# A spectral layer and a token/channel mixer: 940 more columns by seven block products, their groups narrowed earlier and partly on GpSimd

## The chip, the core and the metric

The kernel runs on one core of a Trainium2 chip. The core has a matrix engine (TensorE, in the profile PE for matmuls and PEld for weight loads), VectorE (DVE), ScalarE (ACT), GpSimd (POOL) and a queue processor, SyncE (SP), that here only issues DMAs. SBUF is on-chip memory with 128 partitions, PSUM holds matmul results. The metric is the device time of one execution in microseconds; the kernel before takes 2310.04 us, the median of three runs (2308.27 to 2310.43).

## What is computed

Two parts follow each other, on x of shape (8 batches, 3008 positions, 256 channels):

```python
X = np.fft.rfft(x, axis=1)
Yr = Xr @ w_r - Xi @ w_i + b_r
Yi = Xr @ w_i + Xi @ w_r + b_i
Y = soft_threshold(Yr, 0.01) + 1j * soft_threshold(Yi, 0.01)
y = np.fft.irfft(Y, n=3008, axis=1)            # a
h = np.maximum(y.T @ w_tok1, 0) @ w_tok2       # over positions, 3008 -> 256 -> 3008
u = y + h.T
out = u + np.maximum(u @ w_ch1, 0) @ w_ch2     # over channels, 256 -> 1536 -> 256
```

The weights of the second part arrive as float64. They are read as pairs of 32-bit words and narrowed on the chip to float32 (`narrow`): two ScalarE operations and six that were all on VectorE.

## The kernel before

A position n is written by two indices, of 47 and of 64, and the Fourier transform is done as two short transforms by matmul (`stage1`, `forward`, `inverse`). Where full float32 precision is wanted, an operand is split into a high part in float32r and the remainder, and a product is three matmuls (`mm3`); the split is a copy (mostly ScalarE) and a subtraction (VectorE or GpSimd).

The batches are worked in five units: batch 0 alone, batch 1 alone, then three pairs (`UNITS`, line 24). The *spectral work* of a unit gives blocks b_d in DRAM and a matrix g (the relu of the token product, as gh and gl). From these, a *group* of up to 470 positions of u is made by `half_u`, once for each half of the 256 channels: six matmuls with the group's piece of w_tok2 (tile wt2: high and low parts of two halves, 470 or 376 columns) and one product with a block of b_d (tile b2) for each slot of 94 positions. Unit 0 has seven groups of 470, 376, 376, 376, 470, 470 and 470 columns. For unit 0 the piece of w_tok2 is loaded as float64 (`load_wt2`), narrowed (`narrow_wt2`), split (`split_wt2`), used, and kept in DRAM (`keep_wt2`, tensor wt2_d); the later units load it from there.

The *channel mixing* takes u in chunks of columns. A chunk up to 512 columns wide is done by `channel`: 12 blocks f of the 1536 hidden values, each with a first product (6 matmuls, PSUM tile ph), a relu on ScalarE (hh) and its remainder on VectorE (hlo), and two steps later a second product (6 matmuls, accumulated in PSUM tile po): 144 matmuls. A wider chunk is done in the tail by `channel7`: its columns and the hidden blocks are cut into halves, and a 2 x 2 block product is made with seven products instead of eight in each layer. A step is one of 6 pairs of hidden blocks: seven products of three matmuls for the first layer and seven for the second, 42 matmuls over half the chunk's columns. The sums of columns (tiles t and ub) are made by `first_u`, `rest_u` or `sums_u`, the sums of weights (ws, ws2) by `weigh` and `weigh2` during the last narrow chunk, and `replace` puts sums in place of a quarter of the weights.

Before the change unit 0 has seven narrow chunks, one for each group; unit 1 has wide chunks of 960, 1024 and 1024 columns, each pair 896 and five of 1024.

The order of the work is this:

- `begin` (line 774): the spectral work of batch 0 in plain float32, the narrowing of w_tok1, w_ch1 and of the first pieces of w_ch2, group 0, and the first steps of unit 1's spectral work (each `extra(1)`).
- The loop at line 1445 goes through the narrow chunks. After each step f of `channel` it takes as many steps of the spectral work as a pace asks: the unit-1 work left over the channel work left, from the first chunk to the one ahead of the last narrow one. Unit 1's steps also carry the first transform of unit 2 (`jobs`).
- Ahead of the last narrow chunk ("end") the rest of the spectral work, units 2 to 4, runs by itself, with `wc["pure"]` set; in it `mix` takes its PSUM from the pool ps1 under the tag po.
- Then comes the last narrow chunk, with the sums of weights, and the tail.

In a narrow chunk n the group of the next chunk is prepared at fixed steps: loads at f = 1 and 3, narrowing at 3 and 5, splits at 4 and 6, `make_u` at 9. In the last narrow chunk the three groups of the first wide chunk are made at f = 4, 7 and 10. Outside the tail the framework orders the instructions on each engine by their dependencies and its own estimates when the program is built; in the tail PE keeps the order that is written (ORDER and TURN in `channel7`: O for products of the second layer of the step before, N for the first layer of the new step). Group halves stand between the tail's steps, at places listed in `when`; the tiles wt2 and b2 have one buffer each. Loads run on SP's queue, most stores on ScalarE's (PUT).

## Time and profile before

| what | us |
| --- | --- |
| median of three runs | 2310.04 |
| profiled execution | 2313.43 |
| its span in the trace | 2311.2 |
| PE busy (matmul) | 2273.5 (98%) |
| DVE busy | 1718.8 (74%) |
| ACT busy | 1476.2 (64%) |
| POOL busy | 1389.7 (60%) |

Busy time is from the page of the profiled execution. Matmuls overlap and their ends are modelled, so a busy PE is not PE at its peak; the price of a matmul is better read from the distance between the starts of two. In time the stages lie as follows, by the last relu of the first layer and the last addition of each chunk: `begin` up to 155 us, the first six narrow chunks with unit 1's spectral work to about 446, the spectral work alone to about 858, the last narrow chunk to 906, the tail to the end. Rows of the order of time give start, length, engine, line, operation, output and inputs, shapes, and in brackets the idle time ahead with what ended it; rows of waits give total, times and the longest; rows of groups give count, busy time, mean nanoseconds, idle time.

### The profile page before, as it was taken

To read this page: it belongs to the slowest core of one execution; us is meant where nothing else is said; L and a number is where in the kernel's file an instruction comes from. 1 tells how busy PE (TensorE), PEld (TensorE's weight loads), DVE (VectorE), ACT (ScalarE), POOL (GpSimd) and SP (SyncE) were. 2 spreads that over 40 slices of the span, in tenths; PEclk is the share of its full clock that TensorE was granted. 3 is DMA by queue.
4 is the path that set the end of the run, shared out by engine and by line. 5 is a ranking of instruction groups with operands and counts; after the bars stand their busy time and mean duration, and the time that the engine had idled before them with its cause. 6 is when DMAs were issued, how large, how long until landed. Compare 5 with 4: busy or idle time off the path is not lost.

```text
span 2311.2 us, 34802 instructions
## 1 busy us (share of the span) xinstructions
PE 2273.5 (98%) x12092; PEld 1976.0 (85%) x12092; DVE 1718.8 (74%) x2806; ACT 1476.2 (64%) x2700; POOL 1389.7 (60%) x1119
## 2 busy tenths in 40 slices
PE   8999999999999999999999999999999999999998
PEld 7879999989989988888988888898888889888876
DVE  7967776577887667777777777777777777777877
ACT  6755554455655445776676777667777766767776
POOL 0000223344553333887787888778788877878885
PEclk9999999999999999999999999999999999999999
DMA  8876576787876542122222212222221122222201
GB/s 209 262 241 182 144 215 186 236 260 251 263 241 217 178 153 85 42 81 69 85 62 69 64 37 67 70 85 62 69 65 42 61 69 85 62 69 64 59 1 37
DMA packets 150958, 277.22 MB, mean 120 GB/s; under 512 B 11078, under 2 KB 95390, under 8 KB 150782
## 3 DMA queue, kind: packets, MB, share of 16 engines
q1 hardware_dynamic: 115241, 208.40, 30.2%
q10 hardware_dynamic: 35540, 66.60, 8.5%
q8 instruction: 96, 1.57, 0.3%
q14 instruction: 81, 0.66, 0.1%
HBM read 177.57 MB, written 97.39 MB: 119 GB/s over the span
## 4 chain that ended last, share of the span: by engine, by line
PE 82%; DVE 9%; DMA 3%; issue 2%; ACT 1%; POOL 1%; SPq 1%; ACTq 0%; DVEq 0%; POOLq 0%
PE l L134 15%; PE sx L134 14%; PE sz L134 11%; PE sy L134 10%; PE sw L134 7%; PE px L497 3%; PE pm L208 2%; PE pm L210 2%; PE pm L209 2%; PE gp L210 1%; PE gp L208 1%; PE gp L209 1%; DMA raw<-in_wt 1%; DVE ts L1216 1%; PE gp L578 1%
## 5 line engine op out<-in xcount | busy, mean ns | idle before, releaser
L1213 POOL TENSOR_TENSOR op<-ts,op 128x512 fp32r<-128x512 f32 (+2 forms) x503 | 638.0, 1290 | 245.0 <-ACT op L1246 241.4
L1246 ACT ACTIVATE op<-ts 128x512 fp32r<-128x512 f32 (+2 forms) x504 | 311.2, 619 | 63.5 <-DVE ts L1216 48.2
L1213 DVE TENSOR_TENSOR uf<-sy,uf 128x512 f32<-128x512 f32 (+2 forms) x232 | 156.3, 674 | 223.6 <-PE sy L134 223.2
L134 PE MATMUL l<-op,ws 128*128 128x512 f32 (+2 forms) x1134 | 314.3, 385 | 0.0
L134 PEld LDWEIGHTS l<-op,ws 128*128 128x128 f32 x1134 | 212.9, 188 | 40.1
L1242 ACT ACTIVATE x<-sx 128x512 f32<-128x512 f32 (+2 forms) x252 | 148.5, 589 | 139.2 <-PE sx L134 138.7
L134 PE MATMUL sx<-ub,w 128*128 128x512 f32 (+2 forms) x756 | 211.7, 388 | 1.9 <-DVE ts L1216 1.0
L134 PE MATMUL sx<-ub,ws 128*128 128x512 f32 (+2 forms) x756 | 209.8, 386 | 0.5 <-ACT x L1242 0.5
L161 POOL TENSOR_TENSOR yl<-z,yh 128x512 fp32r<-128x512 f32 x72 | 96.3, 1337 | 126.0 <-ACT yh L158 118.2
L134 PEld LDWEIGHTS sx<-ub,w 128*128 128x128 f32 x756 | 141.7, 188 | 31.5 <-DVE ts L1216 3.2
L134 PEld LDWEIGHTS sx<-ub,ws 128*128 128x128 f32 x756 | 141.8, 188 | 27.8 <-ACT x L1242 0.9
L1213 POOL TENSOR_TENSOR op<-b,op 128x512 fp32r<-128x512 f32 (+2 forms) x126 | 160.8, 1277 | 0.7 <-ACT op L1246 0.2
L1213 DVE TENSOR_TENSOR x<-sw,x 128x512 f32<-128x512 f32 (+2 forms) x126 | 85.7, 680 | 90.4 <-PE sw L134 89.2
L262 POOL TENSOR_TENSOR sd<-x 120x512 f32<-120x512 f32 x39 | 60.8, 1558 | 149.9 <-DVE xl L161 91.2
L208 PE MATMUL pm<-wmh,xth 128*128 128x256 f32 x504 | 145.4, 289 | 3.0 <-DVE z L541 1.7
L1266 ACT ACTIVATE x<-x 128x512 f32<-128x512 f32 (+2 forms) x126 | 78.6, 624 | 108.6 <-DVE x L1213 108.6
L134 PE MATMUL sy<-op,w2h 128*128 128x512 f32 (+2 forms) x464 | 142.2, 388 | 1.0 <-DVE uf L1213 1.0
L210 PE MATMUL pm<-wmh,xtl 128*128 128x256 f32 x504 | 142.4, 283 | 0.0
L209 PE MATMUL pm<-wml,xth 128*128 128x256 f32 x504 | 142.4, 283 | 0.0
L161 POOL TENSOR_TENSOR xtl<-xs,xth 128x256 fp32r<-128x256 f32 x84 | 69.3, 825 | 106.3 <-ACT xth L158 57.9
L161 POOL TENSOR_TENSOR wt<-aw,wt 128x512 fp32r<-128x512 f32 x12 | 16.3, 1360 | 179.6 <-ACT wt L158 179.6
L506 DVE TENSOR_TENSOR xtl<-px,xth 128x512 fp32r<-128x512 f32 x84 | 57.7, 687 | 72.1 <-ACT xth L505 55.2
(225 smaller groups left out, 6684.8 us busy)
## 6 DMA issues: line engine op xcount, KB each, us to landing
wt<-wt_d SPq DMA_DIRECT2D x28, 940.0 KB, 5.8
x<-in_x SPq DMA_DIRECT2D x39, 480.0 KB, 5.7
a<-a_d SPq DMA_DIRECT2D x36, 512.0 KB, 6.1
wt<-ws_d SPq DMA_DIRECT2D x36, 512.0 KB, 5.4
b_d<-bt ACTq DMA_DIRECT2D x36, 512.0 KB, 6.0
a_d<-a ACTq DMA_DIRECT2D x36, 480.0 KB, 4.2
wt<-wt_d SPq DMA_DIRECT2D x21, 752.0 KB, 5.2
b<-b_d SPq DMA_DIRECT2D x32, 480.0 KB, 6.4
```

Source lines behind the costliest of these rows:

```text
L134: return lambda *args, **kw: self.tc.keep_in_program_order(op(*args, **kw))
L161: lo_eng.tensor_tensor(out=lo, in0=src, in1=hi.bitcast(F32), op=ALU.subtract)
L208: PE.matmul(out, lhsT=wh, rhs=xh, start=start, stop=False, skip_group_check=more)
L209: PE.matmul(out, lhsT=wh, rhs=xl, start=False, stop=False, skip_group_check=more)
L210: PE.matmul(out, lhsT=wl, rhs=xh, start=False, stop=stop, skip_group_check=more)
L262: eng.tensor_tensor(out=sd[:, 0], in0=x[:, 0], in1=x[:, 1], op=ALU.add)
L497: PE.matmul(pt[:, o:o + 128], lhsT=x, rhs=f2cols(2 * kp + ab), start=True, stop=True)
L506: V.tensor_tensor(out=v(xl)[:, 1:], in0=both, in1=v(xh)[:, 1:].bitcast(F32), op=ALU.subtract)
L1213: eng.tensor_tensor(out=out, in0=in0, in1=in1, op=op)
L1242: pins[key] = S.activation(out=t, in_=src, func=func)
L1246: pins[k] = S.activation(out=ops[k][:, 0], in_=v[k] if src is None else src, func=AF.Copy if k[0] == "t" else AF.Relu)
L1266: pins["x2r"] = S.activation(out=v["x2"], in_=v["x2"], func=AF.Relu)
```

## The change

Unit 0's last two groups, 470 columns each, become one chunk of 940 columns in the tail. So there are five narrow chunks; the unit-1 spectral work is spread over the first four; groups 5 and 6 are loaded, narrowed and split during chunks 1 and 2 (f = 6 to 13), kept in DRAM during chunks 2 and 3, and loaded again in the last narrow chunk, where their halves are made at f = 4 and 7. Unit 1's three groups of the first 960 columns are made in the first tail chunk: two halves inside its first step (after N5 and N7), the others in and after the next steps.

For groups 1 to 6 the last two operations of `narrow` and the subtraction of the split run on GpSimd; loads stay at f = 1 and 3, narrowing goes to 4 and 6, splits to 5 and 7. The low parts of the sums of weights go from GpSimd to VectorE, and the sums' steps shift.

Smaller edits: unit 1's sums sd use the tag t4 (two buffers, open from the start) instead of the pool wk2; `begin` takes one more spectral step; the load of f1 goes to ScalarE's queue; `prepare_mix` comes after the first two `turn`s, ordered behind the copy of the last one; the first `mix` of the spectral work alone takes ordinary PSUM banks.

```diff
@@ -39,7 +39,7 @@
 SLOW = 1.75
 UNIT1 = NG * SLOW + KP * 5.1 + NG * 3.5
 LAG = 3
-SUMS = (1, 2, 4, 5, 7, 8)
+SUMS = (1, 3, 4, 6, 7, 9)
 
 
 
@@ -165,7 +165,7 @@
 
 
 
-    def narrow(raw, t0, t1, none=None):
+    def narrow(raw, t0, t1, none=None, last=None):
         u0, u1 = t0.bitcast(U32), t1.bitcast(U32)
         lo, hi = raw[..., 0], raw[..., 1]
         low = lo.bitcast(F32)
@@ -178,8 +178,9 @@
         V.tensor_scalar(out=u1, in0=hi, scalar1=0x80000000, scalar2=None, op0=ALU.bitwise_and)
         V.scalar_tensor_tensor(out=u0, in0=u0, scalar=3, in1=u1, op0=ALU.logical_shift_left, op1=ALU.bitwise_or)
         V.tensor_scalar(out=u1, in0=u0, scalar1=0xFF800000, scalar2=None, op0=ALU.bitwise_and)
-        V.tensor_tensor(out=t1, in0=low, in1=t1, op=ALU.mult)
-        V.tensor_tensor(out=t0, in0=t0, in1=t1, op=ALU.add)
+        last = last or V
+        last.tensor_tensor(out=t1, in0=low, in1=t1, op=ALU.mult)
+        last.tensor_tensor(out=t0, in0=t0, in1=t1, op=ALU.add)
         return t0
 
     def load_raw(src, n, pool=None):
@@ -191,13 +192,13 @@
         DMA.dma_start(out=raw.rearrange("p n w -> p (n w)"), in_=src.bitcast(U32))
         return raw
 
-    def load_wide(src, n, pool=None, tag="o", raw=None, after=None):
+    def load_wide(src, n, pool=None, tag="o", raw=None, after=None, last=None):
         if raw is None:
             raw = load_raw(src, n, pool)
         rows = raw.shape[0]
         tmp = wk.tile([rows, 2, n], F32, tag=tag, name="wide", bufs={"o": 3, "hl": 4}[tag])
         if after is None:
-            return narrow(raw, tmp[:, 0], tmp[:, 1])
+            return narrow(raw, tmp[:, 0], tmp[:, 1], last=last)
         wc["none"] = wc.get("none", 4) + 1
         none = wide_sc[:rows, wc["none"]:wc["none"] + 1]
         V.tensor_scalar(out=none.bitcast(U32), in0=after[:rows, :1].bitcast(U32), scalar1=0, scalar2=None, op0=ALU.bitwise_and)
@@ -255,7 +256,7 @@
             return x
         if pool is not None:
             sd = wk.tile([120, 2, w], F32, tag=("xtl", "wt", "et")[g % 3], name="sd", bufs=2)
-        elif "wk2" in wc:
+        elif w > C:
             sd = wc["wk2"].tile([120, 2, w], F32, name="sd", bufs=1)
         else:
             sd = t4([120, 2, w], "sd")
@@ -482,7 +483,7 @@
                     PE.transpose(pt[:, ab * C + t * 128:ab * C + (t + 1) * 128], wc["z"][:, 2 * kp + ab, t * 128:(t + 1) * 128], wc["eye"])
             a2 = ld([128, 2, nb, C], "a2")
             if kp < 2:
-                V.tensor_copy(out=a2.rearrange("p k b c -> p (k b c)"), in_=pt)
+                wc["turned"] = V.tensor_copy(out=a2.rearrange("p k b c -> p (k b c)"), in_=pt)
             else:
                 S.copy(out=a2.rearrange("p k b c -> p (k b c)"), in_=pt)
             return a2
@@ -520,7 +521,7 @@
             return xh, xl
 
         def mix(kp, xt, yh, yl):
-            if "pure" in wc or plain and kp < KP - 1:
+            if wc.get("pure", 0) > 1 or plain and kp < KP - 1:
                 pt = ps1.tile([128, 2, 512], F32, tag=("po", "gp")[kp % 2 if plain else 0], name="pm")
                 p1, p2 = pt[:, 0], pt[:, 1]
             else:
@@ -534,6 +535,8 @@
                         PE.matmul(out, lhsT=x, rhs=wc["mix"][wsel][:, t], start=t == 0, stop=t == 1)
                     else:
                         mm3(out, xt[0][:, j, t], xt[1][:, j, t], wmh[:, wsel, t], wml[:, wsel, t], t == 0, t == 1)
+            if "pure" in wc:
+                wc["pure"] += 1
             z = t4([128, 2, 2, C], "z")
             y, cl = z[:, 0], z[:, 1]
             with tc.issue_after(wc["xs"].ins) if "pure" in wc else ExitStack():
@@ -791,7 +794,7 @@
             wc["early"] = early
             f1w = early.tile([120, 3, 128], F32, name="f1")
             wc["f1"] = f1w[:, :, :120]
-            DMA.dma_start(out=f1w, in_=io["f1"])
+            PUT.dma_start(out=f1w, in_=io["f1"])
             split(f1r[:, 0], f1r[:, 1], f1w[:, :2], S, V)
             wc["eye"] = early.tile([128, 128], F32, name="eye")
             wc["fw"] = early.tile([128, 2, 128], F32, name="fw")
@@ -806,8 +809,9 @@
             V.memset(lam, -LAM)
             for g in range(NG):
                 next(x)
-            prepare_mix()
             a2s = {0: p.turn(0), 1: p.turn(1)}
+            with tc.issue_after(wc["turned"].ins):
+                prepare_mix()
             after = {0: a2s[1][:, 0, 0, :2]}
             w1 = prepare_w1(early, after)
             es, xts = {k: load_e(k) for k in range(2)}, {}
@@ -870,6 +874,7 @@
         done += extra(1)
         make_u(0)
         split_u(0)
+        done += extra(1)
         for r in range(2):
             split_w2(r, f[r])
         return done
@@ -885,7 +890,8 @@
     for u, bs in enumerate(UNITS):
         total, at = N * len(bs), 0
         if u == 0:
-            widths = [k * TOKS for k in sizes[u]]
+            widths = [k * TOKS for k in sizes[u][:5]]
+            widths.append(total - sum(widths))
         else:
             widths = [total % CW7] + [CW7] * (total // CW7)
         for cw in widths:
@@ -912,7 +918,7 @@
     def load_wt2(g, pool=None, parts=(0, 1)):
         u, _, s, k = groups[g]
         cols = slice(s * TOKS, (s + k) * TOKS)
-        if u == 0:
+        if u == 0 and "seven" not in wc:
             for jt in parts:
                 wfs.setdefault(g, {})[jt] = load_raw(io["wt2"][0, jt][:, cols], k * TOKS, pool)
         else:
@@ -922,7 +928,7 @@
 
     def narrow_wt2(g, parts=(0, 1)):
         for jt in parts:
-            wfs[g][jt] = load_wide(None, wfs[g][jt].shape[1], raw=wfs[g][jt])
+            wfs[g][jt] = load_wide(None, wfs[g][jt].shape[1], raw=wfs[g][jt], last=G if g else V)
 
     def keep_wt2(g):
         u, _, s, k = groups[g]
@@ -934,7 +940,7 @@
         if g not in wts:
             wts[g] = wk.tile([128, 4, 480], F32R, name="wt2", bufs=1)
         for jt in parts:
-            split(wts[g][:, jt, :n], wts[g][:, 2 + jt, :n], wfs[g].pop(jt), S, V)
+            split(wts[g][:, jt, :n], wts[g][:, 2 + jt, :n], wfs[g].pop(jt), S, G if g else V)
 
     def load_b2(g):
         u, b, s, k = groups[g]
@@ -1030,13 +1036,18 @@
                     late[f + 1] = f // 2 + 2, narrow_w2(f // 2 + 2)
             if f == 4 and n and n - 1 in mixed:
                 put(n - 1)
+            kept_g = {2: 5, 3: 6}.get(n)
+            if f == 1 and kept_g:
+                keep_wt2(kept_g)
+                del wts[kept_g]
             if after:
                 mine = needs[n + 1]
                 seven = after[2] > CW
                 if f == 1 and seven:
                     yield "rest of it"
                     open_seven()
-                    fetch_g(after[0])
+                    if after[0] != u:
+                        fetch_g(after[0])
                     load_wt2(mine[0])
                     load_b2(mine[0])
                 if f == 2 and not seven:
@@ -1049,15 +1060,21 @@
                     replace((0, f // 4))
                 if seven and f % 4 == 1 and f > 1:
                     replace((1, f // 4 - 1))
+                spare_g = {1: 5, 2: 6}.get(n)
+                if spare_g and f in (6, 8):
+                    load_wt2(spare_g, parts=[f // 2 - 3])
+                if spare_g and f in (9, 11):
+                    narrow_wt2(spare_g, parts=[f // 2 - 4])
+                if spare_g and f in (11, 13):
+                    split_wt2(spare_g, parts=[f // 2 - 5])
                 first_at, apart = (9 if len(mine) == 1 else 4 if seven else 6), (3 if seven else 4)
                 for i, g in enumerate(mine):
-                    if not seven and f in (1, 3, 4, 5, 6):
-                        if f in (1, 3):
-                            load_wt2(g, parts=[f // 2])
-                        if f in (4, 6):
-                            split_wt2(g, parts=[f // 2 - 2])
-                        if f in (3, 5):
-                            narrow_wt2(g, parts=[f // 2 - 1])
+                    if not seven and f in (1, 3):
+                        load_wt2(g, parts=[f // 2])
+                    if not seven and f in (5, 7):
+                        split_wt2(g, parts=[f // 2 - 2])
+                    if not seven and f in (4, 6):
+                        narrow_wt2(g, parts=[f // 2 - 2])
                     if f == 9 and not seven:
                         keep_wt2(g)
                     if f == first_at + apart * i:
@@ -1107,7 +1124,7 @@
         for out, x, y, op in ((s1, a21, a22, ALU.add), (s3, a11, a21, ALU.subtract), (s2, s1, a11, ALU.subtract), (s4, a12, s2, ALU.subtract)):
             V.tensor_tensor(out=out, in0=x, in1=y, op=op)
         ws = wc["ws"][:, 2 * q:2 * q + 2]
-        split(ws[:, :, :, 0], ws[:, :, :, 1], sf, S, G)
+        split(ws[:, :, :, 0], ws[:, :, :, 1], sf, S, V)
 
     def weigh2(q):
         fs = slice(4 * q, 4 * q + 4)
@@ -1123,7 +1140,7 @@
         V.tensor_tensor(out=s3, in0=a11, in1=a21, op=ALU.subtract)
         V.tensor_tensor(out=s4, in0=a12, in1=s2, op=ALU.subtract)
         ws = wc["ws2"][:, 2 * q:2 * q + 2]
-        split(ws[:, :, :, 0], ws[:, :, :, 1], sf, S, G)
+        split(ws[:, :, :, 0], ws[:, :, :, 1], sf, S, V)
 
     def replace(key):
         layer, q = key
@@ -1452,7 +1469,7 @@
             pace, hold = 0.0, left_c - 25.0
         for c in channel(n):
             if c == "end":
-                wc["pure"] = True
+                wc["pure"] = 1
                 for step in sp:
                     if step == "drain":
                         break
```

## The prediction

> **What bounds the kernel now.** I read the page's chain of waits first, then busy time by stretches, then each stretch's order of time.
>
> ```profile
> span 2311.2 us, 34802 instructions
> PE 82%; DVE 9%; DMA 3%; issue 2%; ACT 1%; POOL 1%; SPq 1%; ACTq 0%; DVEq 0%; POOLq 0%
> ...
> 0.00:155.00 155.00, 141.63 (x787) 118.66 (x788) 120.32 (x252) 101.14 (x184) 3.21 (x6) 0.98 0.84 242
> 155.00:446.00 291.00, 284.59 (x1708) 266.15 (x1707) 205.98 (x350) 146.53 (x279) 64.63 (x51) 0.99 0.62 189
> 446.00:684.00 238.00, 234.76 (x1537) 212.77 (x1537) 188.22 (x306) 138.89 (x269) 120.36 (x101) 1.00 0.82 258
> 858.00:906.00 48.00, 46.45 (x244) 40.74 (x242) 35.53 (x57) 20.59 (x42) 14.51 (x6) 1.00 0.41 125
> 906.00:2200.00 1294.00, 1291.06 (x6232) 1099.90 (x6233) 958.69 (x1505) 911.89 (x1631) 1037.92 (x828) 1.00 0.21 65
> ```
>
> Each stretch gives its length, then busy time of PE, weight loads, DVE, ACT, POOL, then PE's granted clock, DMA share, GB/s. The chain is 82% PE, and PE idles only 13.4 us in the start (0 to 155), 6.4 us while the first six chunks run between the spectral steps of unit 1 (155 to 446), 3.2 us in the spectral work alone, 1.6 us in the last narrow chunk, 2.9 us in 1294 us of the tail. So time is won by fewer matmuls, or out of these idle microseconds, and lost where another engine becomes late.
>
> **The change part by part.** *Two narrow chunks become one of seven products.* Price of one 470-column matmul, from PE's order of time in the last narrow chunk, and of one tail step of 480 columns:
>
> ```profile
> 887.44 0.38 PE L208 MATMUL ph<-uh,w 128*128 128x470 f32 x1
> ...
> 894.49 0.38 PE L208 MATMUL pu<-wt,gh 128*128 128x470 f32 x1
> 953.39 0.81 PE L134 MATMUL sy<-ub,w 128*128 128x480 f32 x3
> ...
> 962.51 0.81 PE L134 MATMUL sy<-ub,w 128*128 128x480 f32 x3
> ```
>
> Between the first two rows 33 matmuls start: 7.05/33 = 0.2136 us each. The tail step of 42 matmuls (seven products twice, three matmuls each) takes 9.12 us, 0.217 each, so it runs without gaps. Two narrow chunks are 2 x 144 matmuls, 61.5 us; the new chunk is 6 steps x 42 at 470 columns, 53.8 us: -7.7 us. The products that make u are the same number, only elsewhere. One more chunk boundary costs at most its share of the tail's idle, 2.9/19 = +0.2.
>
> *Narrowing of groups 1 to 6.* The multiply, the add and the low half of the split go from DVE to POOL; the steps from load to narrowing grow from two to three; groups 5 and 6 are prepared in chunks 1 and 2.
>
> ```profile
> L181 DVE TENSOR_TENSOR wide<-raw,wide 128x470 f32<-128x470 f32 x6 | 4.5, 745 | 0.0
> L182 DVE TENSOR_TENSOR wide<-wide 128x470 f32<-128x470 f32 x6 | 4.3, 710 | 0.1
> L161 DVE TENSOR_TENSOR wt<-wide,wt 128x470 fp32r<-128x470 f32 x6 | 4.7, 780 | 1.6 <-ACT wt L158 1.5
> L1012 DVE SCALAR_TENSOR_TENSOR hlo<-ph,hh 128x470 fp32r<-128x470 f32 x36 | 23.1, 643 | 18.3 <-ACT hh L1011 18.2
> ...
> 867.99 3.86 POOL L161 TENSOR_TENSOR ws<-sf,ws 128x768 fp32r<-128x768 f32 x2 [11.46 <-ACT ws L158]
> ```
>
> For three groups of 470 columns DVE loses 4.5+4.3+4.7 = 13.5 us, for three of 376 an estimated 376/470 of it, 10.8: 24 us. The stretch also loses two chunks (61.5 us of PE and two groups of products, some 9.5 us) and shrinks from 291 to about 220 us. DVE: 206 - 24 - two chunks' evictions (24 x 0.643 = 15.4) and splits (estimate 8) = 159 us, 72%. POOL: 64.6 + 36 operations at an estimated 1.1 (768 columns take 3.86/2 = 1.93 us, so 376 and 470 some 0.95 and 1.2) = 104 us, 47%. DMA: 0.62 x 291 = 180 us, less two stores and two loads, about 0.8. The stretch 446 to 684 already runs at DVE 79%, POOL 51%, DMA 0.82, and PE idles 1.4% there. By that rate the new stretch would idle 3 us against 6.4; denser work on one core rarely wins by it, so against this I set the following waits of the interleaved stretch:
>
> ```profile
> DVE hlo L1012 <- ACT hh L1011: 34.0, 22, 6.0
> ACT raw L174 <- DMA raw<-in_wt: 20.5, 7, 4.6
> ACT wt L158 <- DVE wide L182: 13.1, 7, 4.1
> ```
>
> The split's copy on ACT waits for the narrowing's last add. That add now stands on POOL, behind POOL's spectral work, and takes longer; behind the copy on ACT queue the evictions hh, for which DVE (hlo) and then PE wait. The DMA wait of 20.5 us should shrink with the third step. I take +2 us; bounds -3 and +24 (12 copies, each holding PE for 2 us, half of the longest such wait).
>
> POOL and DVE hinder each other here. In the last narrow chunk, in order of time:
>
> ```profile
> 868.25 1.91 DVE L161 TENSOR_TENSOR w<-s,w 128x256 fp32r<-128x256 f32 x1
> ...
> 876.67 0.41 DVE L161 TENSOR_TENSOR w2l<-s,w2h 128x256 fp32r<-128x256 f32 x1
> 870.77 0.48 PE L209 MATMUL po<-hlo,w2h 128*128 128x470 f32 x1 [1.42 <-DVE hlo L1012]
> ```
>
> The same operation takes 0.41 us alone and 1.91 us under the POOL operation of the row at 867.99. The Trainium skill (SBUF — State Buffer, section "SBUF: two separate sides") calls it an exclusive lock: a DVE operation with two SBUF inputs and a GpSimd operation block each other for the whole instruction. The rows agree with it. By that rule, 36 new POOL operations block DVE for up to 36 x 1.1 = 40 us; DVE would stand at 199 of 220 us instead of 159. That speaks against the move, but changes the chances rather than the sum.
>
> *Weights' sums in the last narrow chunk.* Six low halves leave POOL (14.5 us there) for DVE: 768 columns at the rate of the 256-column row (0.41) cost up to 1.2 us each, +7 us, while the six collisions, near 1.5 us each, go: about level at 35 us. PE's part shrinks by one group (4.75 us) to 43 us, so DVE stays below it. The 1.42 us wait above should go: -1; bounds -1.4, +3 (DVE late by its 7 us less the 4 it gains).
>
> *Tail's beginning.* The first tail chunk now makes three groups, not two, and two group halves stand in its first step, which before held none:
>
> ```profile
> 906.38 0.93 PE L134 MATMUL sx<-ub,ws 128*128 128x480 f32 x3 [0.52 <-ACT x L1242]
> 910.02 0.92 PE L134 MATMUL sx<-ub,w 128*128 128x480 f32 x3 [0.76 <-DVE sw L1213]
> 912.55 1.47 PE L134 MATMUL sx<-ub,w 128*128 128x480 f32 x3 [0.63 <-DVE ts L1216]
> ...
> 911.00:917.00 6.00, 5.31 (x20) 4.20 (x20) 2.52 (x5) 3.36 (x7) 5.68 (x5) 0.72 0.00 1
> ...
> wt<-wt_d SPq DMA_DIRECT2D x28, 940.0 KB, 5.8
> ```
>
> The first step waits 1.9 us in three places and then runs six microseconds at a clock of 0.72 (1.7 us lost). Two group halves after N5 and N7 fill the first two waits. But wt2 and b2 have one buffer: the next group's load starts when the second half has read them, lands 5.8 us later, and PE, in written order here, needs it after N4, O1 and N1 (3 x 0.64) and their wait: a new wait of up to 3 us, with everything on PE behind it. I take -1; bounds -3.6, +3.
>
> *Spectral work alone.* Its first mix waited for the output bank:
>
> ```profile
> 449.50 0.36 PE L208 MATMUL pm<-wmh,xth 128*128 128x256 f32 x1 [1.30 <-DVE uf L1076]
> ```
>
> It now takes another bank: -1.3; bounds -1.3, 0.
>
> *The start.*
>
> ```profile
> 0.74 0.47 SPq L794 DMA_DIRECT2D f<-in_f  x1
> ...
> 21.98 0.69 DVE L410 TENSOR_TENSOR wsum<-wf 128x512 f32<-128x512 f32 x1 [2.24 <-DMA wf<-in_w_i]
> 24.26 1.23 PE L497 MATMUL px<-f,a 128*128 128x128 f32 x8 [1.88 <-DVE a L485]
> ...
> 40.00:60.00 20.00, 19.06 (x106) 16.59 (x105) 20.00 (x42) 17.13 (x30) 0.00 (x0) 1.00 0.74 202
> ```
>
> The loads on SP move up by 0.47 us, and the turned copies no longer stand behind wsum's DMA. PE's 1.88 us shrink, but from 26 us on DVE sets the pace (20.00 of 20 us), and its work is only reordered: -1; bounds -3, 0.
>
> ```profile
> 139.88 0.43 DVE L262 TENSOR_TENSOR sd<-x 120x256 f32<-120x256 f32 x1 [3.83 <-PE pw L364]
> 145.58 0.39 PE L209 MATMUL p<-xl,f1r 120*128 120x256 f32 x1 [1.27 <-DVE xl L161]
> 147.36 0.39 PE L208 MATMUL p<-xh,f1r 120*128 120x256 f32 x1 [0.92 <-ACT xh L158]
> 155.17 0.43 DVE L178 TENSOR_SCALAR wide<-raw 128x512 uint32<-128x512 uint32 x1 [5.01 <-DMA raw<-in_moe_w_ch]
> 157.60 0.48 PE L209 MATMUL ph<-ul,w 128*128 128x470 f32 x1 [1.92 <-DVE ul L973]
> ...
> 145.00:150.00 5.00, 3.20 (x13) 2.30 (x14) 5.00 (x10) 2.20 (x5) 1.74 (x1) 0.81 1.04 317
> 150.00:155.00 5.00, 5.00 (x33) 4.72 (x32) 0.16 (x1) 2.21 (x4) 0.00 (x0) 0.85 1.05 323
> 155.00:160.00 5.00, 3.08 (x12) 2.35 (x11) 4.36 (x9) 2.69 (x5) 0.00 (x0) 0.83 1.05 375
> ```
>
> Unit 1's sums sd waited for a pool that opens late and has one buffer for them; PE then waited for xl, and DVE's queue stood 5 us at a weight load, with ul, which channel mixing needs first, behind it. In the t4 buffers the sums need not wait for the pool, and their x tiles, whose slots that load reuses, go free sooner; one more spectral step stands before chunk 0. At stake: waits of 1.27+0.92+1.92 = 4.1 us and (0.19+0.15+0.17) x 5 = 2.6 us of clock. DMA is full there (1.05), which speaks against all of it. I take half, -3.5; bounds -7, +1.
>
> Sum: -7.7 +0.2 +2 -1 -1 -1.3 -1 -3.5 = -13.3 us. The profiled execution took 2313.43 us (span 2311.2), 3.4 above the median of 2310.04; so 2300.1 for it, and 2296.7 as median.
>
> **Rivals.** *Waits only move* (0.21): beginning and tail keep theirs because DMA there is full, the dense stretch costs 4: -7.7 +0.2 -1.3 +4 = about -5, 2305. For it: DMA shares near 1; against it: sd's wait has a plain cause in its pool.
>
> *The start and tail clear fully* (0.14): -7.7 +0.2 -1.3 -1 -3.6 -2 -7 = -22.4, 2288. For it: the clock dips hang on just these waits.
>
> *Slower: ACT is held behind POOL* (0.15). The twelve split copies in chunks 0 to 3, at 2 us of PE each, cost 24 us and bring -13.3 -2 +24 = about +9: 2319. It decides from 15.3/12 = 1.3 us a copy on. For it: the 34.0 us row, where hlo already waits for ACT. Against it: most of those waits end before PE needs hh, two steps later, as PE idles 6.4 us in all.
>
> **How the numbers follow.** Forecast 0.50, 2296.7, its own range 2290 to 2303. A measurement of this kernel tells about 0.2%, 4.6 us: faster is below 2305.4, the forecast, the clearing and half of the moved waits: 0.74; within: the rest of these and a mild form of the slower case, 0.13; slower 0.13. The range 2286 to 2313 leaves out the slower case's far half and the extreme of the gains.
>
> **What would show it.** Tail steps of the 940 chunk near 8.97 us, 252 matmuls of it; the interleaved stretch near 220 us with PE idle under 9 us and DVE under 180; no wait for xl before the first p matmuls and clock 1.00 from 145 to 160; one wait for wt at the tail's second step, under 3 us. I am wrong if hh or po waits in chunks 0 to 3 add up to over 10 us, or if the last narrow chunk turns DVE-bound.

## The result, and the profile after

The changed kernel takes 2323.94 us (median of four runs, 2322.65 to 2327.07) against 2310.03 for the kernel before (median of four): ratio 1.0061, 95% interval 1.0049 to 1.0074. It is 13.9 us slower where 13.3 us less was forecast, and lies above the forecast range of 2286 to 2313. The profiled execution took 2325.19 us with a span of 2323.4, against 2313.43 and 2311.2. Two executions at a low clock, one of e4_small (2793.31 us, clock 0.752) and one of the kernel before beside the first experiments (2394.76 us, 0.894), are left out of all comparisons.

The page of the changed kernel (span, chain of waits by engine), then its busy time by stretches; columns as before (length, PE, weight loads, DVE, ACT, POOL, granted clock, DMA share, GB/s):

```profile
span 2323.4 us, 34976 instructions
PE 77%; DVE 4%; DMA 1%; issue 1%; ACT 1%; POOL 0%; DVEq 0%; ACTq 0%
0.00:151.00 151.00, 139.42 (x792) 116.23 (x792) 124.90 (x262) 99.70 (x183) 3.18 (x6) 1.00 0.86 252
151.00:393.00 242.00, 223.50 (x1392) 207.42 (x1393) 177.55 (x277) 131.97 (x257) 114.50 (x89) 0.99 0.71 220
393.00:800.00 407.00, 400.92 (x2628) 363.71 (x2627) 306.76 (x507) 219.09 (x433) 184.72 (x164) 1.00 0.70 224
800.00:844.00 44.00, 42.55 (x217) 37.37 (x216) 33.07 (x62) 20.15 (x38) 1.28 (x1) 1.00 0.41 128
844.00:924.00 80.00, 76.39 (x373) 66.74 (x372) 47.06 (x78) 48.65 (x93) 47.55 (x41) 0.96 0.21 62
924.00:2200.00 1276.00, 1274.34 (x6160) 1086.04 (x6159) 952.77 (x1495) 901.33 (x1613) 1030.44 (x823) 1.00 0.21 64
```

The rows to compare are those of the chunks with unit 1's spectral work: before, 291 us with 6.4 us of PE idle; now 242 us with 18.5. DVE is busy 73% there, so no engine is full; PE is simply late more often.

To see where, I took PE's order of time in both traces: the distance between the starts of two matmuls, less the steady distance for that width (0.2136 us at 470 columns, 0.217 at 480, 0.1745 at 376, 0.120 at 256 in float32r). What is left is PE's loss, idle or at half clock, in us, of one profiled execution each:

| stretch | before | after | difference | forecast |
| --- | --- | --- | --- | --- |
| steady distances of all matmuls | 2222.8 | 2215.3 | -7.5 | -7.7 |
| `begin` and chunk 0 | 22.4 | 19.2 | -3.2 | -4.5 |
| the other chunks with unit 1's work | 9.9 | 24.2 | +14.3 | +2 |
| spectral work alone | 14.2 | 19.2 | +5.0 | -1.3 |
| last narrow chunk | 2.6 | 2.3 | -0.3 | -1 |
| tail | 26.6 | 30.7 | +4.1 | -0.8 |

(The mean distance at 376 columns is nearer 0.173 in both traces; both kernels have 720 matmuls of that width, so the differences stand.) The differences sum to 12.4, the spans differ by 12.2. The saved matmuls are there; the loss stands in the chunks, at the start of the spectral work alone, and at the tail's second step. The waits in the chunks of the changed kernel (us in total, times, longest):

```profile
POOL wide L182 <- DVE wide L180: 34.1, 4, 28.7
DVE hlo L1018 <- ACT hh L1017: 15.1, 8, 4.8
ACT wt L158 <- POOL wide L183: 12.3, 6, 4.2
ACT raw L174 <- DMA raw<-in_wt: 5.9, 3, 3.1
PE ph L209 <- DVE hlo L1018: 3.4, 3, 1.9
PE po L210 <- DVE hlo L1018: 3.4, 5, 1.3
PE po L209 <- ACT hh L1017: 2.5, 2, 1.4
PE p L209 <- DVE z L543: 1.7, 2, 1.2
PE gp L211 <- POOL wt L161: 1.5, 1, 1.5
PE ph L209 <- ACT uh L974: 1.3, 1, 1.3
PE pm L209 <- DVE hlo L1018: 1.1, 1, 1.1
PE p L209 <- DVE xs L508: 1.1, 1, 1.1
```

The eight PE rows have different causes, 16.0 us together and none over 3.4. ScalarE's copy does wait for GpSimd's add, 12.3 us in six waits; the slower rival had put 2 us of PE on each of twelve copies. And VectorE's wait for hh, on which that rival rested, fell from 34.0 us in six chunks to 15.1 in four. Some DVE operations got longer (groups of the changed kernel in the chunks; count, busy us, mean ns):

```profile
L264 DVE TENSOR_TENSOR sd<-x 120x512 f32<-120x512 f32 x15 | 17.3, 1150 | 0.2
L161 DVE TENSOR_TENSOR ul<-uf,uh 128x752 fp32r<-128x752 f32 x3 | 4.3, 1422 | 0.1
L182 POOL TENSOR_TENSOR wide<-raw,wide 128x376 f32<-128x376 f32 x6 | 7.7, 1281 | 39.8 <-DVE wide L180 32.2 <-issue 3.6 <-PE p L211 2.3
```

Before, the same sd took 752 ns and the same ul 936:

```profile
L263 DVE TENSOR_TENSOR sd<-x 120x512 f32<-120x512 f32 x16 | 12.0, 752 | 0.2
L161 DVE TENSOR_TENSOR ul<-uf,uh 128x752 fp32r<-128x752 f32 x3 | 2.8, 936 | 0.0
```

It would be easy to lay both on the operations moved to GpSimd. For sd the experiments below contradict it. The same groups in e1_dve, where the narrowing is back on VectorE, and sd in e8_poolbefore, the kernel before with the narrowing on GpSimd:

```profile
L264 DVE TENSOR_TENSOR sd<-x 120x512 f32<-120x512 f32 x15 | 18.5, 1233 | 0.1
L161 DVE TENSOR_TENSOR ul<-uf,uh 128x752 fp32r<-128x752 f32 x3 | 2.8, 934 | 0.0
...
L264 DVE TENSOR_TENSOR sd<-x 120x512 f32<-120x512 f32 x15 | 11.3, 750 | 0.3
```

In the changed kernel four of the fifteen sd met no GpSimd operation and took 677 to 682 ns; two met one and took 691 and 692 ns; nine took 1033 to 1790 ns, all beside one, but in seven of these it was only GpSimd's share of the spectral work. So sd grew mostly because the order now puts it beside GpSimd's spectral work. Only the growth of ul goes with the moved operations: two of the three met them (1497 and 1826 ns), the third met none (942 ns).

### The profile page after: what moved, and what is told of

Same layout as the page of the kernel before. It is cut to its first block, busy times and chain, and to the rows that moved or that the text cites. A ratio compares the mean times of both kernels' runs of the same rounds, so it can differ in the third digit from the quotient of the medians.

```text
span 2323.4 us, 34976 instructions
## 1 busy us (share of the span) xinstructions
PE 2270.9 (98%) x12056; PEld 1968.7 (85%) x12056; DVE 1737.9 (75%) x2824; ACT 1504.0 (65%) x2754; POOL 1471.2 (63%) x1192
## 4 chain that ended last, share of the span: by engine, by line
PE 77%; DVE 4%; DMA 1%; issue 1%; ACT 1%; POOL 0%; DVEq 0%; ACTq 0%
PE l L134 15%; PE sx L134 14%; PE sz L134 12%; PE sy L134 10%; PE sw L134 8%; PE px L498 3%; PE pm L209 2%; PE pm L211 2%; PE pm L210 2%; PE gp L211 1%; PE gp L209 1%; PE gp L210 1%; DVE ts L1233 1%; PE pi L209 1%; DVE ub L160 1%; PE pi L210 1%
## 5 line engine op out<-in xcount | busy, mean ns | idle before, releaser
L1230 POOL TENSOR_TENSOR op<-ts,op 128x512 fp32r<-128x512 f32 (+3 forms) x527 | 666.6, 1287 | 291.5 <-ACT op L1263 287.8
L1263 ACT ACTIVATE op<-ts 128x512 fp32r<-128x512 f32 (+3 forms) x528 | 325.2, 618 | 65.9 <-DVE ts L1233 50.0
L1230 DVE TENSOR_TENSOR uf<-sy,uf 128x512 f32<-128x512 f32 (+3 forms) x243 | 163.0, 671 | 237.5 <-PE sy L134 237.0
L134 PE MATMUL l<-op,ws 128*128 128x512 f32 (+3 forms) x1188 | 328.7, 385 | 0.0
L1259 ACT ACTIVATE x<-sx 128x512 f32<-128x512 f32 (+3 forms) x264 | 155.3, 588 | 145.7 <-PE sx L134 145.2
L134 PE MATMUL sx<-ub,w 128*128 128x512 f32 (+3 forms) x792 | 220.8, 387 | 1.7 <-DVE ts L1233 1.6
L134 PE MATMUL sx<-ub,ws 128*128 128x512 f32 (+3 forms) x792 | 219.9, 386 | 1.1 <-ACT x L1259 1.1
L1230 POOL TENSOR_TENSOR op<-b,op 128x512 fp32r<-128x512 f32 (+3 forms) x132 | 167.9, 1272 | 1.8 <-ACT op L1263 1.3
L134 PE MATMUL sy<-op,w2h 128*128 128x512 f32 (+3 forms) x486 | 149.1, 388 | 1.0 <-DVE uf L1230 1.0
L134 PEld LDWEIGHTS sz<-g,b 96*128 96x128 f32 x896 | 115.2, 193 | 3.5 <-DMA b<-b_d 0.6
```

Source lines behind the costliest of these rows:

```text
L134: return lambda *args, **kw: self.tc.keep_in_program_order(op(*args, **kw))
L1230: eng.tensor_tensor(out=out, in0=in0, in1=in1, op=op)
L1259: pins[key] = S.activation(out=t, in_=src, func=func)
L1263: pins[k] = S.activation(out=ops[k][:, 0], in_=v[k] if src is None else src, func=AF.Copy if k[0] == "t" else AF.Relu)
```

## The experiments

The theories at the start: (A) GpSimd's part of the narrowing holds ScalarE and blocks VectorE; (B) unit 1's spectral work is too dense over four chunks; (C) the extra preparation of groups 5 and 6 costs in chunks 1 and 2; (T) the one buffer of wt2 and b2 stalls the tail's second step. Later came (O): any other order of the interleaved work costs or wins some 10 us by itself. The runs up to e15_oldsteps were read without O in mind, so a difference of some 10 us among them doesn't price a cause by itself. "Loss" below is PE's loss as in the table, of the profiled execution; "chunks" are those with unit 1's spectral work, 0 to 3 with the 940 chunk and 0 to 5 without. Chunks and stretch alone have 13.8 and 14.2 us in the kernel before, 28.7 and 19.2 after.

**e1_dve**: narrowing and split back on VectorE.

```diff
-            wfs[g][jt] = load_wide(..., last=G if g else V)
+            wfs[g][jt] = load_wide(..., last=V)
-            split(..., wfs[g].pop(jt), S, G if g else V)
+            split(..., wfs[g].pop(jt), S, V)
```

> The changed kernel, with the last two operations of the narrowing and the low half of the split of groups 1 to 6 back on VectorE. Theory A (GpSimd in the chain of the narrowing holds ScalarE and blocks VectorE): the interleaved stage loses most of its 23 us of PE idle, total 2305 to 2311 us. Theory B (the spectral work is too dense over four chunks, whoever narrows): VectorE is only fuller, 2319 to 2328 us. Theory C (the extra narrowing of groups 5 and 6 in chunks 1 and 2): 2318 to 2326 us.

Measured 2314.57 us (2313.52 to 2316.75), ratio to the kernel before 1.0018 (1.0008 to 1.0027): 9.4 us better than the change, but between the range of A and those of B and C, so none of the three is met. Loss in the chunks 20.0, alone 19.3.

**e2_pace**: the pace of the kernel before; the rest of unit 1's work goes to the stretch alone.

```diff
-            left_c = mixing(0, first_wide - 1)
+            left_c = mixing(0, first_wide - 1) + 67.2
```

> The changed kernel, with the pace of the spectral work beside the narrow chunks as it was before (67.2 us added to the channel work that the pace divides by); what is left of unit 1 runs in the stage of spectral work alone. Theory A: the narrowing's chain stays, 2317 to 2324 us. Theory B: the stalls between 195 and 407 us go and the stage alone grows by the work that moved, 2302 to 2310 us. Theory C: 2316 to 2324 us.

Measured 2336.98 (2334.15 to 2340.17), ratio 1.0114 (1.0098 to 1.013): 13 us slower than the change and above all three expectations. The chunks lose 15.4, the stretch alone 40.8. Its busy time by stretches:

```profile
151.00:331.00 180.00, 169.39 (x1015) 158.91 (x1014) 132.88 (x214) 93.79 (x183) 72.53 (x60) 1.00 0.62 186
331.00:430.00 99.00, 83.22 (x545) 75.80 (x544) 64.83 (x101) 50.59 (x101) 44.36 (x38) 0.92 0.88 281
```

Unit 1's spectral work without channel mixing beside it leaves PE idle for 15.8 of 99 us, at a clock of 0.92. So thinning the chunks by this much is no remedy.

**e3_nospare**: groups 5 and 6 aren't prepared; later units read other columns of w_tok2 in their place (the edit of the load is left out here).

```diff
-            kept_g = {2: 5, 3: 6}.get(n)
+            kept_g = None
-                spare_g = {1: 5, 2: 6}.get(n)
+                spare_g = None
```

> The changed kernel without the load, narrowing, split and store of groups 5 and 6 in chunks 1 to 3; whatever reads their columns of the kept weights reads group 0's columns instead, so that work is left out and nothing else moves. Theory A: a third of the GpSimd operations go, 2315 to 2319 us. Theory B: 2316 to 2323 us, from less DMA alone. Theory C: 2303 to 2309 us.

Measured 2320.51 (2314.4 to 2321.95), ratio 1.0034 (1.0022 to 1.0047): 3.4 us better than the change, far above the range of C and inside that of B. A difference of this size is less than what a new order alone does (e16 to e18), so C has no price from it.

**e4_small**: the kernel before with the small edits alone (sd in t4, f1 on ScalarE's queue, `prepare_mix` later, one more spectral step in `begin`, the first mix's bank).

> The kernel before with the small edits alone: f1's load on ScalarE's queue, the mix weights prepared after the first turned copies, unit 1's sums in the t4 buffers, one more spectral step ahead of chunk 0, ordinary PSUM banks for the first mix of the spectral work alone. By the prediction's terms (-1, -3.5, -1.3): 2304 us, with the clock at 1.00 between 145 and 160 us. If these stalls only move to the next wait: 2308 to 2311 us.

Measured 2308.9 (median of nine, 2304.53 to 2315.92), ratio 0.9996 (0.9986 to 1.0007): nothing that can be measured.

**e5_tail**: e1_dve, with the second group's first half after step 1 of the tail, and the third group's halves after step 3 and inside step 4.

```diff
-                spots = [(ns[0], p) for p in ['N5', 'N7', (1, 'N1'), 1, 2, 3][-2 * len(mine):]]
+                spots = [(ns[0], p) for p in ['N5', 'N7', 1, 2, 3, (4, 'N1')]]
```

> The changed kernel with its narrowing kept on VectorE (2314.57 us in the runs so far) and one more edit: in the first tail chunk the second group's first half is made after step 1 and not inside it, the third group's two halves after step 3 and inside step 4. Theory T (the tail's beginning lost about 3 us because the second group's load, into the one buffer of wt2 and b2, starts only when the first group's second half has read it, and TensorE needs it 5 us later): the wait for wt at the tail's second step goes, the excess of the first two steps falls by 1.5 to 3 us, time 2311.5 to 2313. Rival (the load is late because the DMA queues and the clock dip at the tail's beginning set it, not the order): the first two steps keep their time or the wait moves to another step, time 2314 to 2315.5.

Measured 2310.13 (2307.08 to 2314.46), ratio 0.9997 (0.9986 to 1.0008), 4.4 us better than e1_dve, below the range of T. The wait itself, in the changed kernel, PE's order of time and the windows around it:

```profile
849.44 0.92 PE L134 MATMUL sx<-ub,ws 128*128 128x470 f32 x3 [1.11 <-ACT x L1259]
856.65 0.90 PE L134 MATMUL sx<-ub,w 128*128 128x470 f32 x3 [0.69 <-DVE ts L1233]
859.22 0.66 PE L134 MATMUL sz<-wt,gh 128*128 128x470 f32 x2 [1.66 <-DMA wt<-wt_d]
860.89 2.30 PE L134 MATMUL sz<-g,b 96*128 96x94 f32 x10 [0.16 <-DMA b<-b_d]
...
857.70:861.10 3.40, 1.72 (x8) 1.26 (x8) 0.01 (x1) 0.76 (x2) 3.40 (x4) 1.00 0.71 176
861.10:867.90 6.80, 6.80 (x23) 6.08 (x23) 0.65 (x1) 1.68 (x3) 0.17 (x1) 0.50 0.01 2
```

and the same place of e5_tail, where the load has a step's time:

```profile
855.00:861.00 6.00, 6.00 (x30) 5.30 (x29) 5.94 (x11) 5.10 (x9) 3.31 (x4) 1.00 0.01 3
861.00:867.00 6.00, 6.00 (x35) 5.41 (x34) 1.75 (x4) 2.40 (x5) 2.94 (x3) 1.00 0.00 0
```

T holds: the wait of 1.66 us is gone, and with it 6.8 us at half clock (3.4 us lost). All five traces with the 940 chunk and the old spots have the wait, 1.62 to 1.82 us; none of the eight with the new spots has it. The half clock follows it in four of the five, once for 6.8 us and three times for 3.4, so its size in the changed kernel's trace is in part chance. The tail's first 17 us lose 2.9 us in every kernel with the new spots, 4.7 to 5.6 us in those without.

**e6_fast**: e1_dve with `left_c` smaller by 20.

> The changed kernel with its narrowing on VectorE, and the spectral work of unit 1 paced to be done 20 us of channel mixing earlier, so that later units' spectral steps already run in chunk 3. Theory B2 (spectral work of unit 1 needs channel mixing beside it to fill TensorE's waits; two chunks less leave 61 us less of it, and what stands alone at the start of the spectral stretch costs the 5 us seen there): the start of the spectral stretch falls back from 19.3 to about 14 us beyond its matmuls, chunks 0 to 3 rise by 0 to 3 us, time 2309 to 2313. Rival (the density of spectral steps in the chunks is what costs): chunks 0 to 3 rise from 20 to 25 us or more beyond their matmuls, time 2317 to 2322.

Measured 2319.66 (2315.67 to 2323.26), ratio 1.0031 (1.0019 to 1.0044), as the rival had it. Chunks 28.9, alone 11.3: what the stretch alone wins, the chunks lose.

**e7_density**: the kernel before with `left_c` smaller by 67.2, as dense in its first chunks as the changed one.

> The kernel before with one edit: its pace counts 67.2 us less of channel mixing, so that unit 1's spectral work runs as densely in its first four chunks as in the changed kernel, and chunks 4 and 5 take steps of the next units. Nothing else differs. Theory B2 (two chunks less of channel mixing beside unit 1's spectral work cost 6 to 11 us, wherever that work lies): chunks 0 to 3 rise from 11 us beyond their matmuls to 17 to 22 us as in the changed kernel, time 2313 to 2319. Rival (the density is harmless and the loss in the changed kernel comes from its extra groups, its order and its small edits): chunks 0 to 3 stay at 11 to 13 us, time 2307 to 2312.

Measured 2321.96 (2319.12 to 2323.45), ratio 1.004 (1.0025 to 1.0056); chunks 0 to 3 lose 26.0 instead of 11.0, more than the theory had. This looked like B proved; e16 to e18 below take it back.

**e8_poolbefore**: the kernel before, narrowing and low halves of groups 1 to 6 on GpSimd, nothing else.

> The kernel before with one edit: of the narrowing of groups 1 to 6, the multiply, the add and the low half of the split run on GpSimd, at the steps where they stood. Theory A (GpSimd in that chain holds ScalarE's copies and blocks VectorE, at any density): 6 to 10 us slower as in the changed kernel, 2316 to 2321. Rival A2 (it costs only where the stretch is dense; before, VectorE was busy 71% and had room): 0 to 4 us slower, 2310 to 2314. If moving it there were a gain by itself, 2304 to 2308.

Measured 2322.53 (2320.24 to 2325.02), ratio 1.0043 (1.0029 to 1.0056), 11 us slower though VectorE had room, just above the range of A (stretch from 155 to 446 of this kernel, then its waits):

```profile
155.00:446.00 291.00, 277.73 (x1623) 258.09 (x1624) 186.03 (x302) 139.90 (x267) 100.64 (x83) 0.98 0.60 180
...
DVE hlo L1013 <- ACT hh L1012: 50.0, 27, 6.3
ACT wt L158 <- POOL wide L183: 26.5, 11, 4.4
```

Here the waits of the slower rival stand as they were drawn: ScalarE's copies wait 26.5 us for GpSimd (13.1 for VectorE before), and VectorE's wait for hh rises from 34.0 to 50.0. VectorE is busy 186 us instead of 206, and it doesn't help.

**e9_late**: e5_tail, with groups 5 and 6 prepared late in the stretch alone (hooks at its spectral steps 170 to 216 of 239).

> The kernel with the new tail spots and the narrowing on VectorE (2310.13 us), with one more edit: groups 5 and 6 are loaded, narrowed, split and stored not in chunks 1 and 2 but late in the spectral work alone (some 700 to 785 us, where the profile of that kernel shows VectorE at 68%, the DMA share at 0.53 and 0.42 and TensorE without a gap). Theory D (chunks 0 to 3 are too dense, and part of the load there is the preparation of two extra groups): the excess over TensorE's own time in chunks 1 and 2 falls from 11.5 to 5 to 8 us, the late stretch stays full, time 2304 to 2308. Rival (the two groups cost nothing in chunks 1 and 2; the density is the spectral work's alone, and the preparation costs as much in the late stretch): 2309 to 2313.

Measured 2318.07 (2312.9 to 2322.97), ratio 1.0039 (1.0026 to 1.0052). The time is above both ranges. Half of D came: chunks 1 and 2 lose 5.3 instead of 11.5. But the stretch alone loses 25.8 instead of 17.9, partly in the new place (PE is idle 6.1 us between 650 and 710, where it wasn't before).

**e10_split** and **e11_muladd**: e5_tail with only the low half of the split, or only multiply and add, on GpSimd.

> The kernel with the new tail spots and the narrowing on VectorE (2310.13 us), with only the low half of the split of groups 1 to 6 put back on GpSimd; multiply and add stay on VectorE. Theory A1 (what costs is the chain load - VectorE - GpSimd - ScalarE: ScalarE's copy of the high half waits for GpSimd's add, and hh and hlo queue behind it): the low half stands at the end of the chain and holds nobody, so 2308 to 2312, and ScalarE's waits for GpSimd at the split stay away. Rival A3 (what costs is every GpSimd operation that runs against VectorE's): a third of the 9.4 us, 2312.5 to 2314.5.

> The kernel with the new tail spots and the narrowing on VectorE (2310.13 us), with only multiply and add of groups 1 to 6 put back on GpSimd; the low half of the split stays on VectorE. Theory A1 (ScalarE's copy waits for GpSimd's add): nearly the whole 9.4 us come back, 2317 to 2321. Rival A3 (every GpSimd operation costs alike): two thirds, 2315 to 2317. If only the low half costs (it waits for ScalarE on GpSimd's queue, ahead of the spectral work): 2309 to 2312.

Measured 2320.76 (2313.91 to 2323.59), ratio 1.0041 (1.0028 to 1.0053), and 2315.79 (2311.54 to 2320.83), ratio 1.0024 (1.0014 to 1.0034). The low half at the chain's end costs 10.6 us, above both ranges, the other part 5.7, as A3 had it, and all together 12.3 (next): the prices don't add, so neither A1 nor A3 stands as a sum. A1 also erred in that the low half holds nobody: in e10_split VectorE and ScalarE wait 7.1 us, in seven waits, for it before the next narrowing, and in e5_tail they don't.

**e12_alltail**: the changed kernel with the new tail spots alone.

> The changed kernel with one edit, the new tail spots; narrowing stays on GpSimd as changed. If the causes add up: 2323.9 less the 4.4 us that the spots brought with the narrowing on VectorE, 2318 to 2321. If the tail's gain in that comparison was another order of the work by chance: 2322 to 2325.

Measured 2322.4 (2318.09 to 2326.34), ratio 1.005 (1.0031 to 1.0068). The tail's first 17 us lose 2.9 instead of 5.0 as in e5_tail, yet the median falls by 1.5 us only. That is in the second range; as single times run from 2318 to 2326, the first isn't excluded.

**e13_hold**, **e14_pace15**, **e15_oldsteps**: e5_tail with the spectral steps starting after 10 instead of 25 us of mixing; with `left_c` larger by 15; with narrowing at f = 3 and 5 and splits at 4 and 6 as before.

> The kernel with the new tail spots and the narrowing on VectorE (2310.13 us), whose spectral steps begin 10 us instead of 25 us of channel mixing into chunk 0. Density theory (what costs is many spectral steps for each us of channel mixing): the same steps over 15 us more of mixing, 7% less dense, 0.5 to 3 us faster, 2307 to 2309.5. Rival (chunk 0, where w2 is still split and the DMA queues are full, can't take steps): its excess rises from 4.4 to over 7 us, 2311 to 2315.

> The kernel with the new tail spots and the narrowing on VectorE (2310.13 us), with the pace counted for 15 us more channel mixing, so that some of unit 1's spectral work is left to the stretch alone. 67 us more made 22 us slower, 20 us less made 5 us slower. Density theory: chunks 0 to 3 fall from 21 to 17 us beyond their matmuls, the stretch alone rises by less, 2307 to 2310. Rival (unit 1's spectral work costs more alone than in the chunks, at any amount): 2311 to 2316.

> The kernel with the new tail spots and the narrowing on VectorE (2310.13 us), with narrowing and splitting of each chunk's own group at the steps where the kernel before has them (two steps after the load, one step after that). If the third step between load and narrowing was of use: ScalarE waits for the load's DMA again (20.5 us before, in seven waits), and 2311 to 2314. If the DMA has no part in the loss: 2308.5 to 2311.5.

Measured 2321.93 (ratio 1.0052, 1.0033 to 1.007), 2321.28 (1.0046, 1.003 to 1.0062) and 2309.09 (0.9997, 0.9988 to 1.0007). The first two are 11 to 12 us slower than e5_tail and above both of their ranges, though both make the steps thinner, where density would have them faster; the third step between load and narrowing was of no use.

**e16_plus5**, **e17_minus5**, **e18_minus34**: the kernel before, one number changed.

```diff
-            left_c = mixing(0, first_wide - 1)
+            left_c = mixing(0, first_wide - 1) + 5.0     # or - 5.0, - 33.6
```

> The kernel before, its pace counted for 5 us more channel mixing (steps 2% less dense). Density theory: no change that can be measured, 2308 to 2312. Rival (any other order of the same work costs, since the pace in place happens to fit): 2314 to 2322, with waits at other places in each order.

> The kernel before, its pace counted for 5 us less channel mixing (steps 2% denser). Density theory: 0 to 1.5 us slower, 2309 to 2313. Rival (any other order costs): 2314 to 2322.

> The kernel before, its pace counted for 33.6 us less channel mixing, half of e7_density's 67.2, which made 10.6 us slower. Density theory: about half of that, 3 to 7 us slower, 2313.5 to 2318, and chunks 0 to 3 between the 11 and 26 us of idle beyond their matmuls of the kernel before and of e7_density. Rival (any other order costs): no such grading, as slow as e7_density or as fast as the kernel before.

Measured 2322.05 (2320.19 to 2325.52), ratio 1.0051 (1.0035 to 1.0067); 2319.79 (2318.18 to 2323.39), 1.0041 (1.0025 to 1.0058); 2305.82 (2303.78 to 2310.54), 0.9981 (0.9971 to 0.9992). The first two are where the rival had them (the first by 0.05 us above), the third is faster than either expectation. There is no grading: +5 costs 12 us, -5 10 us, -33.6 wins 4 us, -67.2 costs 11 us. Density as such is not the price, and O fits all three. The stretch from 155 to 446 in e18_minus34, the best, then in e16_plus5; in the kernel before PE was busy 284.59 us there, VectorE 205.98, and the DMA share was 0.62:

```profile
155.00:446.00 291.00, 285.10 (x1751) 268.38 (x1751) 222.98 (x365) 153.02 (x294) 76.82 (x60) 0.99 0.70 209
155.00:446.00 291.00, 279.59 (x1651) 261.84 (x1652) 199.32 (x334) 138.35 (x264) 62.33 (x47) 0.98 0.59 176
```

The fuller stretch leaves PE idle for 5.9 us, the emptier one for 11.4.

One thing that such an order does is seen in e16_plus5, in its order of time, ScalarE, VectorE and PE at 224 us, and in its PE waits from 155 to 446:

```profile
224.21 0.54 ACT L172 ACTIVATE wide<-raw 128x376 f32<-128x376 f32 x1 [5.19 <-DMA raw<-in_wt]
224.21 0.36 DVE L178 TENSOR_SCALAR wide<-raw 128x376 uint32<-128x376 uint32 x1 [6.81 <-DMA raw<-in_wt]
227.34 0.43 PE L208 MATMUL po<-hh,w2h 128*128 128x376 f32 x1 [2.71 <-ACT hh L1011]
...
PE po L209 <- DVE hlo L1012: 5.2, 3, 2.2
PE ph L209 <- DVE ul L973: 3.1, 1, 3.1
PE po L208 <- ACT hh L1011: 2.7, 1, 2.7
```

In this order the narrowing of a late load stands in ScalarE's and VectorE's queues ahead of hh. Both queues stand 5.2 and 6.8 us, PE 2.7 us behind them, and a window at half clock follows at 227.7. Why the order of e18_minus34 is a good one wasn't traced.

## Why the prediction was wrong

*The seven-product chunk* was right: -7.5 against -7.7. A step without group halves takes the forecast 8.97 us, 42 matmuls of 0.2136 (changed kernel, order of time):

```profile
901.88 0.80 PE L134 MATMUL sy<-ub,w 128*128 128x470 f32 x3
910.85 0.81 PE L134 MATMUL sy<-ub,w 128*128 128x470 f32 x3
```

*The interleaved stretch* is the step that failed. PE's work in it was sized well: by steady distances chunks 0 to 3 hold 212.8 us, where 291 - 61.5 - 9.5 less PE's 6.4 idle gives 214. Its loss was not: +14.3 us against +2 (inside the bound of +24). My +2 was set between a gain of 3 us, by the rate of idling of another stretch, 446 to 684, and 24 us for the waiting copies. So it took idling as a matter of the engines' load plus one named chain, and put the new order at nothing. The runs show that idling doesn't follow the load: with five paces the kernel before spreads over 2305.8 to 2322.1 us, and an emptier stretch idled more than a fuller one. The order in place before, 6.4 us idle in 291, was one of the good ones, and the change replaced it. So the forecast should have carried some +7 us (the four other paces average 2317.4), and a spread of about 16, for an order not yet known. How much of the 14.3 us is order, how much GpSimd and how much the two extra groups stays open: each experiment that took one of them away also laid down a new order.

*Narrowing on GpSimd.* The 36 operations took 43.6 us (forecast 40), and of VectorE's operations beside them ul grew, from 936 to 1422 ns. The Trainium skill (SBUF — State Buffer, section "SBUF: two separate sides") has a VectorE operation with two SBUF inputs and a GpSimd operation that reads SBUF blocking each other for whole instructions; the rows of ul and sd agree. But sd is longer on average in e1_dve (1233 ns) than in the changed kernel (1150), so the collisions of sd, the larger part, don't explain what the move to GpSimd cost. Every comparison with this part on GpSimd came out slower: 9.4 us (change and e1_dve), 11.2 (e8_poolbefore), 12.3 (e12_alltail and e5_tail), 10.6 and 5.7 for its parts. But a pace moved by 5 us costs as much, so no single one of these proves its price. Taken as families of orders, without e2_pace (the slowest), e4_small, e10_split and e11_muladd: five orders of the kernel before without it average 2315.9 us (before, e7, e16, e17, e18), seven with the 940 chunk and VectorE 2316.4 (e1, e5, e6, e9, e13, e14, e15), four with GpSimd 2322.3 (after, e3, e8, e12). The saved 7.5 us don't show in the means, and GpSimd stands six microseconds higher. With single orders 16 us apart, and three of the four GpSimd kernels at one pace, both are estimates and not shown. That ScalarE waits behind GpSimd is shown in e8_poolbefore; what this costs the kernel stays open. The slower rival, 2319, had the nearest time, in part by luck: its chain is real, but in the changed kernel it carried 12.3 us of ScalarE's waits, and PE's waits have eight causes.

*The tail's beginning* (-1, bounds -3.6 and +3): the whole tail came to +4.1. The new wait was forecast as up to 3 us and was 1.66 for wt and 0.16 for b; but the gains that I set against it failed, since x and ts still end waits of 1.11 and 0.69 us there, and I left out the clock: the wait brought 6.8 us at half speed. e5_tail shows the wait and its clock by taking them away. The six microseconds at a clock of 0.72 that the prediction tied to the first step's waits were chance: six other traces with the narrow chunks (e4, e7, e8, e16, e17, e18) have the same three waits, 0.52, 0.76 to 0.88 and 0.62 to 0.98 us, and none has half clock there.

*The first mix* (-1.3) got its bank, but the stretch alone lost 5.0 us more: px waits for ScalarE, which waits for a store (changed kernel, order of time):

```profile
406.05 1.07 ACT L285 COPY a<-p 120x512 f32<-120x512 f32 x2 [5.67 <-DMA a_d<-a]
406.69 1.73 PE L498 MATMUL px<-f,a 128*128 128x128 f32 x8 [3.11 <-ACT a L285]
```

*The start and the stretch from 142 to 160* (together -4.5) brought -3.2, and its clock stayed at 1.00 as forecast, though p still waits 1.47 us for xl. That was luck: e4_small, e1_dve and e5_tail have the same edits, and their traces show half clock from 147.6, 154.2 and 155.0 us on. e4_small is also no faster over its runs, so the gain is one of this execution, not one of the edits. *The last narrow chunk* (-1) brought -0.3; VectorE is busy 33.07 of 44 us there, so it isn't bound. Of my own signs, hh and po waits of PE came to 9.3 us, just under the 10 set; PE idle of 18.5 instead of under 9 was the sign that spoke, and the stretch took 242 us instead of 220.

The loss stands partly in the clock: its mean over the changed kernel's four runs is 0.9955, so 10.5 us of the span are lost at half clock; over the kernel before's runs 5.2 us. Of the 13.9 us, some 5 are clock.

## What to carry to other kernels

Where a program lays down each engine's order from its own estimates, any edit there is also a new draw of the order: move one pacing number to both sides and time it before believing a difference of half a per cent, and give a forecast of such an edit that spread. When an operation got longer beside another engine's, look whether it did so too in a run without the moved work. Separate what an edit does by count (matmuls saved, a wait in a written order) from what it does by order; here the matmul term was right to 0.2 us, and the interleaved stretch outweighed it. A draw can also be used: the kernel before with its pace at -33.6 is the best of all that ran, 2305.82 us, ratio 0.9981 (0.9971 to 0.9992).

## What the hardware showed

*Half a window idle is enough for half the clock.* The granted clock changes on a fixed grid of 3.41 us in each trace. Laid over all twenty traces (30 to 2290 us), with PE's idle time summed in each window at full clock (the ends of matmuls are modelled), it gives this: all 48 windows with 1.81 us idle or more were followed by half clock; of 65 between 1.40 and 1.81 us 13 were; of 13030 below 1.40 one was (1.29). Windows of the changed kernel, each with its next (the second number is PE's busy time; the rest of 3.40 is idle):

```profile
140.90:144.30 3.40, 1.93 (x14) 1.60 (x13) 3.33 (x7) 2.20 (x5) 0.00 (x0) 1.00 1.07 271
144.30:147.70 3.40, 3.40 (x24) 3.15 (x23) 2.71 (x7) 0.38 (x1) 0.70 (x1) 1.00 0.98 302
267.20:270.60 3.40, 1.47 (x10) 1.27 (x9) 3.40 (x6) 0.64 (x2) 1.18 (x1) 1.00 0.59 142
270.60:274.00 3.40, 3.40 (x11) 3.11 (x10) 3.29 (x8) 0.64 (x2) 0.94 (x1) 0.50 0.89 260
```

1.47 us idle left the clock at 1.00, 1.93 halved it. The Trainium skill (TensorE: Matmul & The Clock Gate, section "What's actually happening") gives the window as 3413 ns, which agrees, and the return to the lower clock after at least one idle window; here a window idle for little more than half did it. So a stall of 1.8 us in one window costs a further 1.7 us for each window at half clock that follows, and by these counts the same stall, split by the grid's edge into two parts below 1.4 us, nothing more. That fits the spread between executions of one kernel, though where the grid falls in the executions without a trace wasn't seen.

*The order moves the time as much as the change does.* Some three per cent of one pacing number (5 us of the 157 of channel mixing that are left when the steps begin; e16_plus5, e17_minus5) move the time by 0.4 to 0.5%, with the same 12092 matmuls and one VectorE instruction more or less.
